# Loading the first constants ahead of the first q, with a new written-out order for ten steps

## The chip, the cores and the metric

The kernel runs on one core of a Trainium2 chip. The metric is the device time of one execution in microseconds. Times of the kernel before are the median of three runs; the profile and its trace come from one further execution of their own.

A core has five engines that the profile names PE (TensorE, matrix products), DVE (VectorE), ACT (ScalarE), POOL (GpSimd) and SP (SyncE, which here does nothing but issue transfers). PEld is the loading of a product's stationary operand. Each engine works through its own list of instructions in order; semaphores make one wait for another. A row "SPq" is the issue of a transfer, not the transfer.

## The reference

Two parts follow each other. The first is a gated linear recurrence, per batch and head, over 768 tokens with heads of 48 elements:

```python
batch, n_heads, seq, head_dim = (4, 8, 768, 48)
f = 1.0 / (1.0 + np.exp(-f_logit))
for t in range(S):
    state = f[:, :, t, :, None] * state + np.einsum('bhd,bhe->bhde', k[:, :, t], v[:, :, t])
    y[:, :, t] = np.einsum('bhd,bhde->bhe', q[:, :, t], state)
```

The second takes the 3072 tokens of 384 elements that come out, lets a gate choose one of eight experts for each, and runs that expert's two layers on it:

```python
logits = x @ w_gate
expert_idx = np.argmax(logits, axis=1)
...
    h = np.maximum(x_sorted[lo:hi] @ w1[e], 0.0)
    y_sorted[lo:hi] = h @ w2[e]
y = y_sorted[inv_perm]
return (gate_w[:, None] * y).astype(np.float32)
```

Everything is in 32-bit floats.

## The kernel before

**Units.** The recurrence is computed in chunks of 128 tokens. A unit is one chunk of two batches; there are twelve (NU = 12), and units alternate between two pairs of batches, so that unit u follows unit u - 2. A unit has 8 segments of 128 columns, in two halves a and b, one for each batch: four pairs of heads, with the two heads of a pair at partitions 0 and 64.

**Steps of a unit.** Each step has a short name, with the unit's number and, where it is done for half a unit, a or b behind it:

- lf, lk, lq, lv (SyncE): load f, k, q, v of the unit. f of units 0 and 1 is loaded in halves.
- exp, ln (ScalarE): the logarithms of the gates; sum (VectorE): their running sum (a scan); r and dec (ScalarE): the sum's exponential, and that of its negative.
- kr (POOL, L560): k times r. krv is the same product on VectorE. krx is kr with one dependency more: it also waits for the latest q, oh or place of VectorE that was written out ahead of it.
- q (VectorE, L583): q times dec.
- sc (TensorE, L594): scores k by q, 16 small products for a half, into two of four PSUM banks.
- mx, my (VectorE, L600): copy the scores under the causal mask, which frees the banks.
- kp (TensorE, L607): transposes of k against the identity; keep (ScalarE, L610) copies them out.
- wi (TensorE, L618): masked scores by v, into one of the two banks yt, one for each half. bef (L639): the old state's part, added into the same banks. set (ScalarE, L681) copies a bank out, after which the next unit's wi may begin in it.
- dp (TensorE, L655): what the unit adds to the state; upd (VectorE, L669 and L671) adds it, and updp (POOL, L673) scales it by the last decay, which last (POOL) has copied.
- xp (TensorE, L717): turns the output into rows and computes the gate's logits, against wx. lg (VectorE) sums the logits, lay (ScalarE) copies the rows.
- line (POOL), oh, place (VectorE), ex (ScalarE), send (POOL): choose the expert for a group of two units, count, find each row's place, and scatter the rows into the buffer xs with indirect transfers, two scatters for each send.

The results of kp, dp, xp and the counts take turns in two PSUM banks. Buffers for loads: four for q, three for k, two for f, three for v; three for the gates and decays.

**Constants.** `_consts()` packs all constants into one array fpack, of which the identity is the first 128 columns, and the mask into mpack. `load_first_consts()` (L164, step consts0) issues the transfers of the identity and the mask, 64 KB and 16 KB; `load_consts()` (L175, step consts1) those of the rest. The transposes kp need the identity as an operand; sel0 (L168, POOL) copies pieces of it into wx; the masks need mpack.

**Warm-up products.** `warm(count)` (L751, step fill) issues products of the cleared tile pad with itself into a bank that the first wi overwrites. Their result isn't used. Each is two records in the trace.

**The order.** Inside `tc.manual_schedule` each engine's instructions stand in the order in which they are written. For the first ten steps of the pipeline the order is written out by hand in the string FIRST_STEPS: a loop takes it word by word and calls what stands under that name in the table DO, with the unit and the half. A word sets its place only against the other words of its own engine. Units 10 and 11 and the end of the routing follow from the loop at L897, where ordered code takes the place of the words. Behind it stands the second part: the rows of each expert are read back from xs, turned, and multiplied by w1 and w2 (L337 and L353); the first two experts' first tiles are read back early, as soon as certain scatters have landed, and their products (PE s L337) begin inside the first part, near 117 us.

Of the kernel before, what the change touches and what calls it, by code (L numbers as in the profile page):

```python
# [121 lines left out]
def kernel(  # L122
# [305 lines left out]
    def load_pads(e):  # L428
# [12 lines left out]

    FIRST = 10
    FIRST_STEPS = """
        lf0a exp0a ln0a fill24 lf0b exp0b lk0 ln0b sum0a dec0a sum0b ends0 lf1a lq0 lf1b r0a
        r0b exp1a krv0a krv0b consts0 kp0a lk1 ln1a q0a sc0a lq1 exp1b ln1b dec0b keep0a
        sum1a sel0 fill8 dec1a r1a sum1b r1b kr1a q0b q1a kp0b kr1b keep0b lf2 lv0 lf3 lk2
        lv1 mx0a my0a lq2 sc0b mx0b my0b last0 dp0 upd0 sc1a exp2 ln2 wi0a gate0 lf4 kp1a
        dec1b lk3 lq3 lv2 kp1b ends1 sum2 ends2 q1b exp3 lf5 wi0b set0a keep1a last1 mx1a
        sc1b my1a mx1b r2 krx2 consts1 keep1b dp1 my1b wi1a set0b kp2a upd1 kp2b dec2 q2 ln3
        sum3 ends3 exp4 ln4 upd0p upd1p sc2a mx2a sc2b keep2a keep2b my2a last2 dec3 line0  # L450
        r3 xp0a xp0b set1a lq4 wi1b last3 lg0a lay0a mx2b my2b set1b wi2a wi2b dp2 lg0b krv3
        bef2 line1 line2 lk4 lv3 lf6 pads0 lk5 lv4 lay0b kp3a exp5 ln5 sum4 r4 q3 exp6 sc3a
        sc3b upd2 krx4 upd2p kp3b mx3a my3a keep3a xp1a dec4 mx3b my3b keep3b xp1b lg1a q4
        lg1b last4 lay1a dp3 sum5 lq5 lay1b sc4a sc4b ends4 ends5 oh1 kp4a upd3 lf7 set2a
        wi3a set2b wi3b mx4a my4a mx4b ln6 kp4b lk6 r5 kr5 dec5 q5 keep4a xp2a lv5 keep4b
        bef3 exp7 lg2a xp2b lay2a set3a set3b dp4 lq6 lf8 lk7 sum6 sc5a lg2b lay2b my4b
        ends6 dec6 upd4 ex1 place1 ln7 wi4a q6 sc5b lv6 r6 upd3p kp5a kp5b lq7 last5 last6
        mx5a kr6 lf9 wi4b lk8 lv7 keep5a line3 xp3a keep5b xp3b my5a sc6a mx5b upd4p my5b
        sc6b lg3a exp8 ln8 lay3a lg3b lay3b bef4 oh3 lq8 set4a lf10 set4b send5 sum7 r7 krx7
        dec7 last7 dp5 kp6a sum8 upd5 wi5a ends7 ends8 mx6a my6a mx6b wi5b bef5 kp6b line4  # L460
        lk9 keep6a xp4a keep6b q7 my6b set5a lv8 lq9 ex3 xp4b dec8 lg4a lg4b lay4a sc7a q8
        wi6a lay4b r8 place3 send6 dp6 upd6 kp7a sc7b mx7a my7a mx7b set5b line5 wi6b keep7a
        kp7b xp5a my7b krx8 sc8a exp9 ln9 keep7b xp5b exp10 ln10 lg5a sum9 lg5b oh5 lay5a
        lay5b lf11 bef6 upd5p last8 upd6p set6a set6b dp7 kp8a keep8a r9 wi7a upd7 kp8b
        keep8b lk10 sum10 kr9 mx8a my8a upd7p line6 xp6a lg6a ex5 sc8b ends9 exp11 mx8b dec9
        last9 q9 lay6a xp6b lg6b ends10 my8b lay6b place5 lv9 lq10 line7 dec10 q10 lk11
        last10 wi7b bef7 set7a set7b sc9a dp8 kp9a upd8 lv10 wi8a wi8b send7 r10 kr10 sc9b
        send8 lq11 lw0 lww0 lv11 lw1 ln11 mx9a lww1 kp9b keep9a keep9b upd8p xp7a xp7b send9
        bef8 my9a mx9b lg7a lay7a dp9 sum11 r11 lg7b lay7b my9b oh7 upd9
    """  # L470

    with ExitStack() as st:
# [891 lines left out]
```

## Time and profile before

| what | time |
|---|---|
| median of three runs | 391.99 us (391.94 to 394.16) |
| the profiled execution | 388.52 us |
| its span, first to last instruction | 386.5 us |
| first warm-up product starts | 1.57 us |
| first transpose kp0a starts | 11.03 us |
| last work of unit 9 (dp9) ends | 96.96 us |
| first expert product (PE s L337) starts | 117.50 us |

The page's rows of forty slices show how the engines share the span; a digit is the busy share of a slice in tenths, a slice is 9.66 us:

```profile
PE   8899999999999999999999999999999999999993
DVE  6899989897874632122121131116412113111360
ACT  6899885884532000010100110000010000001000
POOL 4444256658946310201002102100210210210112
```

The first part of the kernel takes the first twelve slices or so; there all four engines are used. From the thirteenth on TensorE works nearly alone, on the experts. Its granted clock has the digit 9 in all forty slices.

In the timeline rows below, the columns are the start in microseconds, the busy time, the engine with the line, operation and operands, the number of instructions merged into the row, and in brackets the idle time before it with what ended it. In rows of waits, the engine and line that waited stand left of the arrow, then what it waited for, with the total in microseconds, the number of waits and the longest.

### The profile page before, as it was taken

The page shows a single profiled execution, that of the slowest core. Times are in us where ns is not written, and L with a number is a line of the kernel's source. Part 1 is how long each engine was busy: PE and PEld are TensorE (multiplying, and loading weights), DVE is VectorE, ACT ScalarE, POOL GpSimd, SP SyncE. Part 2 cuts the span into 40 slices and gives each one's busy share as a digit, 9 for nine tenths or more (in the row PEclk, how much of TensorE's full clock was granted, in tenths as well). Part 3 has the DMA queues.
Part 4 walks back from the last instruction along what each step waited for, and adds up shares of the span by engine and source line. Part 5 has one row for each costly group of instructions (what it writes and reads, how often), then busy time and mean ns, then how long its engine had stood idle before and what let it go on. Part 6 is the DMA issues. An engine that isn't in the chain of part 4 may idle for free.

```text
span 386.5 us, 7693 instructions
## 1 busy us (share of the span) xinstructions
PE 377.2 (98%) x3054; PEld 264.6 (68%) x3054; DVE 170.2 (44%) x367; ACT 102.3 (26%) x190; POOL 98.9 (26%) x120
## 2 busy tenths in 40 slices
PE   8899999999999999999999999999999999999993
PEld 8789988889989777685555555654466466455452
DVE  6899989897874632122121131116412113111360
ACT  6899885884532000010100110000010000001000
POOL 4444256658946310201002102100210210210112
PEclk9999999999999999999999999999999999999999
DMA  7999765759993559594649999898163369993141
GB/s 260 388 360 372 261 230 199 249 181 303 412 354 123 174 162 333 118 344 77 197 130 396 264 392 395 221 398 220 41 247 113 102 211 385 397 415 138 21 175 54
DMA packets 51659, 94.81 MB, mean 245 GB/s; under 512 B 20840, under 2 KB 40875, under 8 KB 49568
## 3 DMA queue, kind: packets, MB, share of 16 engines
q1 hardware_dynamic: 48448, 84.62, 64.5%
q0 software_dynamic: 3168, 9.64, 6.6%
q8 instruction: 25, 0.41, 0.4%
q14 instruction: 18, 0.15, 0.1%
HBM read 79.23 MB, written 15.21 MB: 244 GB/s over the span
## 4 chain that ended last, share of the span: by engine, by line
PE 85%; DMA 6%; issue 2%; POOL 2%; DVE 1%; SPq 1%; ACT 1%; POOLq 0%; ACTq 0%; DVEq 0%
PE hps L337 28%; PE yps L353 24%; PE yps L1143 7%; PE s L594 5%; PE yt L618 4%; PE xp L717 3%; DMA xs<-xr,posi 3%; PE s L337 3%; PE hps L1117 3%; PE yp L353 3%; PE kp L607 2%; DMA fpack<-c_fpack 2%; PE dp L655 2%; PE yt L639 1%; DMA xrow<-xs 1%
## 5 line engine op out<-in xcount | busy, mean ns | idle before, releaser
L337 PE MATMUL hps<-xT,w1t 128*128 128x352 f32 (+2 forms) x384 | 110.1, 447 | 0.0
L337 PEld LDWEIGHTS hps<-xT,w1t 128*128 128x128 f32 x384 | 72.7, 190 | 37.2 <-issue 1.9
L353 PE MATMUL yps<-w2t,hT 128*128 128x384 f32 x288 | 94.4, 487 | 0.0
L353 PEld LDWEIGHTS yps<-w2t,hT 128*128 128x128 f32 x288 | 54.6, 190 | 38.6 <-issue 1.5
L196 POOL DMA_INDIRECT out_dram<-ysb,dst x24 | 23.4, 974 | 224.7 <-DVE ysb L364 215.6
L347 ACT ACTIVATE hT<-hps 128x352 f32<-128x352 f32 (+2 forms) x28 | 13.7, 491 | 200.7 <-PE hps L337 200.7
L349 DVE TENSOR_SCALAR hT<-hps 128x352 f32<-128x352 f32 (+2 forms) x28 | 15.6, 558 | 93.0 <-PE hps L337 93.0
L364 DVE TENSOR_SCALAR ysb<-yps,tg 128x384 f32<-128x384 f32 x22 | 13.6, 618 | 74.4 <-PE yps L353 55.7
L600 DVE COPY_PREDICATED at<-mpack,s 128x512 f32<-128x512 uint8 x48 | 32.1, 732 | 3.1 <-PE s L594 3.1
L560 POOL TENSOR_TENSOR k<-k,r 128x1024 f32<-128x1024 f32 (+1 forms) x11 | 25.2, 2296 | 20.5 <-ACT r L556 14.6
L542 DVE TENSOR_TENSOR_SCAN sum<-g,cap 128x1032 f32<-128x1032 f32 (+1 forms) x14 | 28.2, 2022 | 2.2 <-ACT g L535 2.2
L196 POOL DMA_INDIRECT xs<-xr,posi x24 | 25.5, 1063 | 13.7 <-issue 4.6
L1143 PE MATMUL yps<-qw,hqT 128*32 128x192 f32 (+1 forms) x192 | 26.8, 380 | 0.0
L594 PE MATMUL s<-q,k 64*128 64x128 f32 x384 | 26.3, 281 | 0.1
L717 PE MATMUL xp<-wx,ys 128*128 128x104 f32 x192 | 24.9, 279 | 0.2 <-ACT ys L681 0.2
L594 PEld LDWEIGHTS s<-q,k 64*128 64x128 f32 x384 | 22.8, 187 | 2.6 <-issue 1.2
L618 PE MATMUL yt<-at,v 128*48 128x128 f32 x384 | 24.3, 276 | 0.0
L717 PEld LDWEIGHTS xp<-wx,ys 128*128 128x128 f32 x192 | 22.9, 192 | 1.0 <-ACT ys L681 0.3
L618 PEld LDWEIGHTS yt<-at,v 128*48 128x48 f32 x384 | 20.2, 123 | 2.1 <-issue 1.0
L1143 PE MATMUL yps<-w2t,hT 128*32 128x384 f32 x192 | 21.4, 487 | 0.0
L583 DVE TENSOR_TENSOR q<-q,g 128x1024 f32<-128x1024 f32 (+1 forms) x14 | 16.7, 1196 | 1.1 <-DMA q<-in_qu_dram 0.9
L1143 PEld LDWEIGHTS yps<-w2t,hT 128*32 128x32 f32 x192 | 7.6, 110 | 13.0 <-issue 12.5
(116 smaller groups left out, 354.9 us busy)
## 6 DMA issues: line engine op xcount, KB each, us to landing
qw<-in_moe_w_dram SPq DMA_DIRECT2D x16, 1536.0 KB, 12.9
w1t<-in_moe_w_dram SPq DMA_DIRECT2D x8, 1536.0 KB, 7.3
w2t<-in_moe_w_dram SPq DMA_DIRECT2D x8, 1536.0 KB, 15.8
k<-in_ku_dram SPq DMA_DIRECT2D x12, 512.0 KB, 6.1
q<-in_qu_dram SPq DMA_DIRECT2D x12, 512.0 KB, 6.2
f<-in_fu_dram SPq DMA_DIRECT2D x10, 512.0 KB, 6.3
xs<-pad SPq DMA_DIRECT2D x8, 600.0 KB, 3.9
v<-in_vu_dram SPq DMA_DIRECT2D x12, 384.0 KB, 5.1
```

What stands on the lines that cost most here:

```text
L196: ins = nc.gpsimd.indirect_dma_start(out=dst, out_offset=bass.IndirectOffsetOnAxis(ap=idx, axis=0), in_=src, in_offset=None, bounds_check= ...
L337: nc.tensor.matmul(x["h"][:, f], lhsT=w[0][:, j, b * 128 : b * 128 + 128], rhs=x["xT"][:, j], start=j == 0, stop=j == KD - 1,)
L349: nc.vector.tensor_scalar(to, x["h"], 0.0, None, op0=OP.max)
L353: nc.tensor.matmul(yp, lhsT=x["hT"][:, f, t * C : t * C + C], rhs=w[1][:, f, :], start=f == 0, stop=f == NF - 1,)
L542: nc.vector.tensor_tensor_scan(x["sum"][:, part].rearrange("p s c -> p (s c)"), x["g"][:, part].rearrange("p s c -> p (s c)"), cap[:, part ...
L560: ins = on.tensor_tensor(k, k, units[u]["r"][:, part], op=OP.mult).ins
L583: return nc.vector.tensor_tensor(q, q, x["dec"][:, part], op=OP.mult).ins
L594: done["score"] = nc.tensor.matmul(ps[h][:, p], lhsT=x["k"][r, s], rhs=x["q"][r, s], start=True, stop=True).ins
L600: nc.vector.copy_predicated(x["at"][:, a, h], _bc(causal, 1, HP), x["ps", a][h])
L618: nc.tensor.matmul(x["yt"][a][DP * (h ^ a) : DP * (h ^ a) + D, p], lhsT=x["v"][:, a, 2 * p + h], rhs=x["at"][:, a, h, p], start=p == 0, st ...
L717: nc.tensor.matmul(x["xp", a][:, p], lhsT=x["ys", a][:, p], rhs=wx[:, p, 0:XW] if a else wx[:, p, E:WX], start=True, stop=True,)
L1143: nc.tensor.matmul(yp[r], lhsT=h[:, f, at : at + T], rhs=w[:, f, cols], start=f == 0, stop=f == NF - 1, skip_group_check=True,)
```

## The change

It replaces the string FIRST_STEPS and nothing else. The first lines of it:

```diff
-        lf0a exp0a ln0a fill24 lf0b exp0b lk0 ln0b sum0a dec0a sum0b ends0 lf1a lq0 lf1b r0a
-        r0b exp1a krv0a krv0b consts0 kp0a lk1 ln1a q0a sc0a lq1 exp1b ln1b dec0b keep0a
-        sum1a sel0 fill8 dec1a r1a sum1b r1b kr1a q0b q1a kp0b kr1b keep0b lf2 lv0 lf3 lk2
-        lv1 mx0a my0a lq2 sc0b mx0b my0b last0 dp0 upd0 sc1a exp2 ln2 wi0a gate0 lf4 kp1a
...
+        lf0a lf0b exp0a ln0a sum0a exp0b ln0b dec0a fill21 sum0b r0a lk0 krv0a r0b krv0b
+        lf1a consts0 lq0 lf1b kp0a dec0b q0a lk1 q0b sc0a exp1a ln1a sum1a exp1b ln1b sc0b
+        keep0a ends0 kp0b sum1b ends1 lq1 lf2 lv0 dec1a last0 r1a r1b lf3 lk2 lv1 lq2 fill8
+        q1a keep0b dp0 exp2 ln2 krx1a gate0 lf4 mx0a my0a mx0b my0b lk3 lq3 lv2 upd0 dec1b
...
```

Read by engine, this is what it does:

- SyncE: consts0 stands ahead of lq0 and lf1b instead of behind them. Its order is otherwise the same for all 58 steps.
- TensorE: 21 warm-up products at the start instead of 24. The eight others stand behind sc0b and kp0b instead of between sc0a and kp0b.
- The order on TensorE, VectorE, ScalarE and POOL is different in many places up to the last word. TensorE's for units 4 and 5, and ScalarE's around them:

```
before  PE   sc4a sc4b kp4a wi3a wi3b kp4b xp2a bef3 xp2b dp4 sc5a wi4a sc5b kp5a kp5b wi4b xp3a xp3b
after   PE   sc4a kp4a sc4b wi3a kp4b wi3b xp2a xp2b bef3 sc5a dp4 wi4a wi4b kp5a sc5b kp5b xp3a xp3b
before  ACT  exp5 ln5 r4 exp6 keep3a dec4 keep3b lay1a lay1b set2a set2b ln6 r5 dec5 keep4a keep4b exp7 lay2a set3a set3b lay2b
after   ACT  exp5 ln5 keep3a r4 keep3b dec4 lay1a set2a set2b lay1b exp6 dec5 keep4a r5 keep4b ln6 lay2a exp7 exp8 set3a set3b lay2b
```

- POOL: send7, the first send of the second group of units, stands ahead of kr9 instead of behind last9 and last10; send8 stands ahead of kr10 instead of behind it. Of the products k times r, those of unit 1 (both halves) and unit 6 wait in addition for VectorE's latest step (krx), those of units 2, 4 and 7 no longer do; unit 8's does in both.

No step is added or taken away apart from the three warm-up products.

More of the change, by code (lines that the diff above doesn't have):

```diff
@@ L443 @@
     FIRST_STEPS = """
-        lf0a exp0a ln0a fill24 lf0b exp0b lk0 ln0b sum0a dec0a sum0b ends0 lf1a lq0 lf1b r0a
-        r0b exp1a krv0a krv0b consts0 kp0a lk1 ln1a q0a sc0a lq1 exp1b ln1b dec0b keep0a
-        sum1a sel0 fill8 dec1a r1a sum1b r1b kr1a q0b q1a kp0b kr1b keep0b lf2 lv0 lf3 lk2
-        lv1 mx0a my0a lq2 sc0b mx0b my0b last0 dp0 upd0 sc1a exp2 ln2 wi0a gate0 lf4 kp1a
-        dec1b lk3 lq3 lv2 kp1b ends1 sum2 ends2 q1b exp3 lf5 wi0b set0a keep1a last1 mx1a
-        sc1b my1a mx1b r2 krx2 consts1 keep1b dp1 my1b wi1a set0b kp2a upd1 kp2b dec2 q2 ln3
@@ L450 @@
[L450 to L467, printed above, removed]
@@ L468 @@
-        send8 lq11 lw0 lww0 lv11 lw1 ln11 mx9a lww1 kp9b keep9a keep9b upd8p xp7a xp7b send9
-        bef8 my9a mx9b lg7a lay7a dp9 sum11 r11 lg7b lay7b my9b oh7 upd9
+        lf0a lf0b exp0a ln0a sum0a exp0b ln0b dec0a fill21 sum0b r0a lk0 krv0a r0b krv0b
+        lf1a consts0 lq0 lf1b kp0a dec0b q0a lk1 q0b sc0a exp1a ln1a sum1a exp1b ln1b sc0b
+        keep0a ends0 kp0b sum1b ends1 lq1 lf2 lv0 dec1a last0 r1a r1b lf3 lk2 lv1 lq2 fill8
+        q1a keep0b dp0 exp2 ln2 krx1a gate0 lf4 mx0a my0a mx0b my0b lk3 lq3 lv2 upd0 dec1b
@@ new lines @@
+        sc1a exp3 lf5 sum2 krx1b kp1a kp1b consts1 lq4 sel0 keep1a keep1b q1b ends2 wi0a
+        wi0b sc1b last1 r2 kr2 line0 mx1a my1a mx1b dp1 my1b line1 set0a set0b wi1a upd1
+        dec2 q2 ln3 exp4 wi1b sum3 kp2a sc2a mx2a kp2b sc2b my2a mx2b keep2a xp0a lg0a ln4
+        keep2b xp0b line2 dec3 lk4 lv3 set1a lay0a wi2a my2b r3 lg0b set1b dp2 lay0b last2
+        wi2b exp5 ln5 lf6 q3 pads0 krv3 kp3a sum4 keep3a sc3a sc3b upd0p r4 upd2 kp3b xp1a
+        keep3b ends3 mx3a my3a mx3b my3b lk5 dec4 lv4 lq5 ends4 lg1a xp1b lay1a bef2 set2a
@@ new lines @@
+        lg1b dp3 set2b upd1p lf7 q4 kr4 sc4a last3 lay1b kp4a upd2p sc4b lk6 lv5 exp6 sum5
+        lq6 wi3a upd3 kp4b wi3b oh1 dec5 q5 keep4a mx4a r5 xp2a lg2a lf8 last4 last5 ends5
+        my4a mx4b keep4b xp2b lg2b ln6 sum6 kr5 ends6 lk7 upd3p lay2a lv6 bef3 lq7 sc5a exp7
+        exp8 set3a set3b my4b dp4 lay2b dec6 ex1 wi4a wi4b upd4 place1 kp5a line3 last6 r6
+        krx6 q6 mx5a keep5a ln7 upd4p sc5b lf9 kp5b keep5b my5a send5 mx5b xp3a lg3a lay3a
+        xp3b bef4 set4a lg3b lay3b ln8 my5b oh3 sum7 sc6a set4b exp9 r7 dp5 upd5 line4 wi5a
@@ new lines @@
+        wi5b kp6a kp6b keep6a sc6b sum8 mx6a lk8 lv7 lq8 lf10 lk9 lv8 ex3 kr7 my6a keep6b
+        dec7 ln9 xp4a mx6b lg4a my6b xp4b lg4b lay4a lay4b send6 q7 bef5 dp6 dec8 lq9 place3
+        ends7 line5 line6 sc7a mx7a sc7b upd6 r8 kp7a my7a mx7b set5a krx8 wi6a last7 set5b
+        q8 keep7a kp7b upd5p xp5a my7b keep7b xp5b lg5a exp10 lg5b lay5a oh5 upd6p ends8
+        sum9 sc8a ln10 sum10 wi6b bef6 set6a lf11 set6b dp7 upd7 sc8b lay5b kp8a keep8a
+        last8 send7 mx8a wi7a lk10 lv9 wi7b bef7 r9 kr9 dec9 my8a mx8b kp8b dec10 upd7p lq10
@@ L470 @@
+        xp6a keep8b xp6b set7a wi8a r10 my8b lk11 lg6a lay6a ex5 q9 last9 lg6b lay6b ends9
+        ends10 lv10 lq11 q10 sc9a sc9b exp11 send8 place5 dp8 upd8 kp9a set7b ln11 kr10
+        last10 lw0 lww0 keep9a wi8b upd8p kp9b line7 xp7a lv11 lw1 mx9a my9a mx9b keep9b
+        lg7a lay7a bef8 sum11 xp7b r11 lg7b dp9 lay7b send9 my9b oh7 upd9 lww1
     """
```

## The prediction

> **What bounds the kernel now.** I read the page's busy rows first, then TensorE's own waits over the first 120 us, then the timeline of the first 16 us with the SyncE issues, and last the chain of waits near 117 us.
>
> ```profile
> PE 377.2 (98%) x3054; PEld 264.6 (68%) x3054; DVE 170.2 (44%) x367; ACT 102.3 (26%) x190; POOL 98.9 (26%) x120
> ```
> ```profile
> PE yt L754 <- DVE yt L482: 1.6, 1, 1.6
> PE kp L607 <- DMA fpack<-c_fpack: 1.4, 1, 1.4
> PE xp L717 <- ACT ys L681: 0.2, 1, 0.2
> PE s L337 <- DVE xT L320: 0.2, 1, 0.2
> ```
> TensorE is busy for 98% of the span, and these four rows are all its waits in the first 120 us: 1.6 us until a cleared bank is there, 1.4 us for the identity (fpack), and two of 0.2 us. From 11.03 us on it has no other gap. So this stage is worth what its first real product starts earlier, less any stall that the new order makes, and nothing else.
>
> ```profile
> 1.57 8.06 PE L754 MATMUL yt<-pad 128*128 128x128 f32 x48 [1.57 <-DVE yt L482]
> 2.14 0.43 SPq L517 DMA_DIRECT2D f<-in_fu_dram  x1
> 2.61 0.43 SPq L517 DMA_DIRECT2D q<-in_qu_dram  x1
> 3.09 0.43 SPq L517 DMA_DIRECT2D f<-in_fu_dram  x1
> 3.56 1.39 SPq L165 DMA_DIRECT2D fpack<-c_fpack  x1
> 4.99 0.65 SPq L166 DMA_DIRECT2D mpack<-c_mpack  x1
> 10.03 0.69 DVE L583 TENSOR_TENSOR q<-q,g 128x512 f32<-128x512 f32 x1 [0.87 <-DMA q<-in_qu_dram]
> 11.03 0.63 PE L607 MATMUL kp<-fpack,k 128*128 128x128 f32 x4 [1.40 <-DMA fpack<-c_fpack]
> 11.58 1.16 PE L594 MATMUL s<-q,k 64*128 64x128 f32 x16
> ```
> The transposes kp0a (L607) need the identity and start at 11.03; the first scores sc0a (L594) follow at 11.65 in the chain of waits. But sc0a's own operand, q0a, is ready at 10.72: VectorE took it up the moment q of unit 0 landed. Two transfers therefore end nearly together, and the change swaps them.
>
> **The change part by part.**
>
> *The swap.* Issue plus time to landing gives f1a at 8.75 (2.14 + 6.6), q0 at 10.0 (2.61 + 7.4), f1b at 10.7 (ScalarE's wait ends there), the identity at 10.89 (3.56 + 7.33), the mask at 11.1 (4.99 + 6.1). Landings follow the issues, with bytes moving at 350 to 400 GB/s. The identity came 0.17 us after f1b, the mask about 0.2 us later. In front of q0 they cost between 0.2 us (80 KB at 400 GB/s) and 0.37 us (those two steps). The other end: their issues take 1.39 + 0.65 = 2.04 us of SyncE, so q0 is issued near 4.7 instead of 2.61, and if the transfer engines ran dry it would land 2.04 us late. The stretches of 1 us show about 0.86 MB moved by 5.2 us, and 1.36 MB are issued ahead of q0 then, so they don't run dry. I take 0.32: q0 lands at 10.33, q0a is done at 10.33 + 0.69 = 11.02, sc0a starts at 11.06 (0.04 us for the hand-over, as at 25.56 in the chain), against 11.65: 0.59 us gained. Ends: 0.72 gained, 1.13 lost.
>
> *The identity and kp0a.* It lands at about 8.75 + 0.17 = 8.9. 21 products instead of 24 are six records fewer at the end of the warm-up, at 11 a microsecond: it ends near 9.63 - 0.55 = 9.1. kp0a then runs from 9.1 to 9.7, in the shadow of the wait for q0. Without that cover it costs its 0.63 us again. The three products are worth nothing themselves: they stood before a wait.
>
> *The clock.* The records of the warm-up go at 6 to 7 a microsecond until 6.5 us and at 10 to 12 from there; the row PEclk shows full clock throughout and doesn't tell this. [...] Here the release came 4.9 us after the first product, well before the 21st, and a gap of 1.40 us (9.63 to 11.03) was followed by transposes at 273 ns, which is full speed. The new gap, 9.7 to 11.06, is no longer. By the row: nothing. [...] I take the row.
>
> *Up to the second unit.* Old VectorE order q0a sum1a sum1b q0b q1a, new q0a q0b sum1a sum1b q1a: the same five pieces, 0.6 to 0.69 and 1.23 us each. They end at 10.33 + 4.35 = 14.7 (old 14.6), masks for unit 0 to 17.3 without the 0.35 us wait on sc0b that the timeline has at 16.29, sum2, q1b, masks of unit 1 and q2 to 25.1. TensorE from 11.06: sc0a, sc0b (q0b 11.6), kp0b, 8 warm-ups (1.97 us), dp0, sc1a at 16.9 (POOL's kr1a now waits for q1a, 14.7, and takes 1.4: 16.1), ..., sc2a at 25.9. Nothing is late, though VectorE is close. f1b lands 0.3 us later, and ln1b is done at 12.4, before sum1b at 12.8.
>
> *The rest of the ten steps.* Every step keeps its instructions; only orders differ. I laid TensorE's new list end to end with the times from start to start of the old timeline (scores 1.09, within 1.01, before 1.02, dp 1.07, transposes 0.57, rows 0.89 and 0.97), and VectorE's beside it. q is ready before its scores by 1.0 us for unit 4 (39.9 against 40.9), 4.7 for 5, 1.0 for 7, 1.6 for 8. Masks free banks 2 us or more ahead. SyncE's order differs in the constants alone, but a transfer still waits for its buffer: exp6 moves behind set2b and lay1b (about 41.4 instead of 34.96), so f of unit 8 is issued at 42.4 instead of 38.98, with k, v and q behind it in that queue. POOL: kr4, kr5, kr6, kr8, kr9 end 2 us or more ahead of their scores. The wait for VectorE's latest step (krx) goes from kr2, kr4 and kr7 and comes to kr1a, kr1b and kr6, where the identity copies (sel0, needed at 28.6, done near 19) and upd4p and send5 queue behind it; kr6 waits for place1 (53.8) and ends near 56.3, sc6a is at 58.8. I cost all this at 0; the cover is thin at the places named among the rivals.
>
> *The row chain near 117 us.* POOL is full from 81.30 to 106 us, after 5.95 us idle. Its scatters end in rows read back, whose transpose releases TensorE:
> ```profile
> 81.30 2.82 POOL L560 TENSOR_TENSOR k<-k,r 128x1024 f32<-128x1024 f32 x1 [5.95 <-ACT r L556]
> 102.94 1.84 POOL L196 DMA_INDIRECT xs<-xr,posi  x1 [0.17 <-issue]
> 117.50 2.27 PE L337 MATMUL s<-xT,w1t 128*128 128x128 f32 x18 [0.16 <-DVE xT L320]
> ```
> If this chain stayed, TensorE coming 0.59 us early would only wait longer. send7 (two scatters, 2.3 us) moves in front of kr9, into that idle time. kr11 then waits for r11 (about 98.2) instead of starting at 99.45: the chain comes 1.1 us early, more than TensorE's 0.59, and the 0.16 us goes too.
>
> Sum: 0.59 + 0.16 = 0.75, say 0.7 us. The profiled execution took 388.52 us with a span of 386.5; I expect a span of 385.8. The median of the three runs is 391.99, 3.5 above the profiled one, and the difference is put on that: 391.3.
>
> **The rivals.**
>
> *Small stalls give it back.* At kp3b, kp5b, kp7b and kp8b the new list has rows xp right behind. The second rows need ScalarE's copy of those transposes 0.89 us after they end, and the copy takes 0.55 to 0.59: 0.3 us to spare. The old list did this at kp9b (92.40) without a gap, for it; but ScalarE has r or dec in front of some of them, 0.95 us each, against it. Two places half a microsecond late: 391.99 - 0.7 + 1.0 = 392.3. Chance 0.2.
>
> *Slower: exp8 ahead of set3a.* The new ScalarE order is exp7 exp8 set3a. f of unit 8, issued at 42.4, must land by 49.9, that is within 7.5 us, or exp8 holds set3a, and wi4a on TensorE (51.7) waits. f took 5.7 to 7.2 us in this stage, for the change; q took 7.4 and up to 8.3 early on, against. Beyond 7.5 each microsecond is one lost; beyond 8.2 the kernel is slower than before. At 10 us: 391.3 + 2.5 = 393.8. Chance 0.12.
>
> *q0 lands 2 us late*, the other end of the swap: 391.99 + 1.13 - 0.16 = 393.0. The bytes still waiting at 5.2 us speak against it. Chance 0.08.
>
> *The change moves nothing*, since identity and q0 share the same engines and end together again: 391.99. Landings in order of issue speak against it. Chance 0.1.
>
> **How the numbers follow.** Forecast 0.45; the remaining 0.05 is for the clock and stalls I haven't seen. The forecast's own range is 391.0 to 391.9. I give 390.5 to 393.3: below, the most that all TensorE gaps can give (1.40 + 0.18 + 0.16 = 1.74, so 390.3) rounded in; above, the late q0 and a middling exp8 stall. About 1% (3.9 us) is what a measurement of this kernel can tell from no change. More than 1.74 us cannot come out of these gaps, so faster by 1% has 0.02, for the measurement alone; slower by 1% needs four microseconds of stalls, 0.06; within 0.92.
>
> **What would show it.** Right: the identity lands near 8.9, q0 near 10.3, kp0a about 9.1, sc0a about 11.1, no wait of TensorE until 117, where s L337 starts near 116.8 without waiting for xT. Wrong: sc0a after 11.65; a TensorE wait on ys (exp8) near 51.7 or on kn or lg behind a transpose; products at half speed after the gap; a wait on xT of over half a microsecond.

## The result, and the profile after

The change makes the kernel slower: 397.86 us (median of six runs, 396.81 to 398.52) against 391.97 us (six runs, 391.22 to 394.16), a ratio of 1.0139, interval 1.0113 to 1.0165. The profiled execution took 396.81 us with a span of 394.9, 8.4 us more than the one before. 391.3 us was forecast, with a range up to 393.3.

These are the page's rows of forty slices for the changed kernel, of 9.87 us each. TensorE has two dents that it hadn't, in the eighth slice (69.1 to 79.0 us) and the fourteenth (128 to 138), and the granted clock, full throughout before, falls in the ninth:

```profile
PE   8999999699999899999999999999999999999993
PEclk9999999989999999999999999999999999999999
```

TensorE's waits over the first 130 us of the changed kernel (who waited, for what, total in us, times, longest):

```profile
PE s L594 <- POOL k L560: 3.3, 1, 3.3
PE yt L754 <- DVE yt L482: 1.6, 1, 1.6
PE s L594 <- DVE q L583: 0.7, 1, 0.7
PE dp L655 <- issue: 0.6, 2, 0.4
PE dp L655 <- DMA v<-in_vu_dram: 0.4, 1, 0.4
```

The wait for the identity (1.4 us before) is gone; in its place stand 0.7 us for q0. So the front of the change works. But a wait of 3.3 us for k, which GpSimd multiplies, is new and larger than all that could be gained. The timeline of GpSimd in the changed kernel shows what held it:

```profile
65.88 1.04 POOL L196 DMA_INDIRECT xs<-xr,posi  x1 [0.16 <-issue]
67.22 1.81 POOL L196 DMA_INDIRECT xs<-xr,posi  x1 [0.30 <-issue]
69.02 0.21 POOL L566 COPY rend<-sum 128x8 f32<-128x8 f32 x1
75.59 0.19 POOL L702 COPY xr<-fpack 128x4 f32<-128x4 f32 x1 [6.35 <-DMA xs<-xr,posi]
75.71 0.15 POOL L703 MEMSET xr<- 128x56 f32 x1
75.82 2.33 POOL L560 TENSOR_TENSOR k<-k,r 128x1024 f32<-128x1024 f32 x1
78.11 0.19 POOL L578 COPY last<-g 128x8 f32<-128x8 f32 x1
```

L702 is step line6. It writes the token numbers into the row buffer xr of the fourth group of units. There are three such buffers (`bufs=3`), so the fourth group takes the first group's, and that is still the source of the scatters of send5 and send6. The last of these four scatters is issued at 67.22 and, by the chain of waits, lands 8.22 us later; until then line6 waits, 6.35 us. Behind it in GpSimd's queue stands krx8, and for that TensorE's scores sc8a wait, 3.27 us. Before the change line6 stood behind upd7p. The last scatter landed 5.7 us after its issue at 68.42 there, some 12 us before line6 began, and kr8 had run by then. From GpSimd's timeline of the kernel before:

```profile
71.14 2.37 POOL L560 TENSOR_TENSOR k<-k,r 128x1024 f32<-128x1024 f32 x1 [1.03 <-DVE xr L275]
85.87 0.22 POOL L702 COPY xr<-fpack 128x4 f32<-128x4 f32 x1
```

TensorE's timeline of the changed kernel, before and behind that wait:

```profile
72.91 2.03 PE L717 MATMUL xp<-wx,ys 128*128 128x104 f32 x16
78.21 1.42 PE L594 MATMUL s<-q,k 64*128 64x128 f32 x16 [3.27 <-POOL k L560]
79.57 1.95 PE L618 MATMUL yt<-at,v 128*48 128x128 f32 x16
81.44 1.52 PE L639 MATMUL yt<-q,state 48*48 48x128 f32 x32
82.90 1.14 PE L655 MATMUL dp<-v,kn 128*64 128x48 f32 x32
```

The three groups behind the wait take 1.42, 1.95 and 1.52 us where the same groups take 1.16, 1.08 and 1.09 elsewhere: 1.56 us more. The view of stretches, with TensorE's busy time (and instructions), the granted clock, the transfer engines' share and GB/s, tells why; the changed kernel:

```profile
74.00:78.00 4.00, 0.94 (x8) 1.00 0.41 136
78.00:80.00 2.00, 1.79 (x20) 0.74 0.00 0
80.00:82.00 2.00, 2.00 (x28) 0.50 0.00 0
82.00:84.00 2.00, 2.00 (x62) 0.90 0.65 183
```

In steps of half a microsecond the mean clock is 0.97 in the step from 78.5, 0.50 in the six that follow and 0.62 in the step from 82.0. So TensorE had half its clock from 78.97 to 82.38 us, 3.41 us. The wait is paid for twice: while it lasts, and in the slow work behind it.

In the two profiled executions the last work of unit 9 ends at 102.67 instead of 96.96 us, 5.7 later; the wait and the slow work behind it make 4.8 of that. The other 2.7 us of the span come later: 1.5 in the fourteenth slice, where TensorE waits for ScalarE's hT (the experts' first-layer output), the rest in small gaps. The experiments tell whether those belong to the change.

### The profile page after: what moved, and what is told of

Same layout as the page of the kernel before. It is cut to its first block, busy times and chain, and to the rows that moved or that the text cites. A ratio compares the mean times of both kernels' runs of the same rounds, so it can differ in the third digit from the quotient of the medians.

```text
span 394.9 us, 7686 instructions
## 1 busy us (share of the span) xinstructions
PE 379.7 (96%) x3048; PEld 266.2 (67%) x3048; DVE 172.6 (44%) x367; ACT 102.3 (26%) x190; POOL 112.1 (28%) x120
## 4 chain that ended last, share of the span: by engine, by line
PE 87%; DMA 5%; POOL 3%; issue 2%; DVE 0%; ACT 0%; SPq 0%; POOLq 0%
PE hps L337 28%; PE yps L353 24%; PE yps L1143 7%; PE s L594 5%; PE yt L618 5%; PE xp L717 4%; PE s L337 3%; PE yp L353 3%; PE hps L1117 3%; PE yt L639 2%; DMA xs<-xr,posi 2%; PE kp L607 2%; PE dp L655 2%; DMA v<-in_vu_dram 2%; DMA f<-in_fu_dram 1%
## 5 line engine op out<-in xcount | busy, mean ns | idle before, releaser
L196 POOL DMA_INDIRECT xs<-xr,posi x24 | 30.7, 1279 | 16.5 <-issue 4.6
L618 PE MATMUL yt<-at,v 128*48 128x128 f32 x384 | 25.3, 281 | 0.2 <-ACT ys L681 0.2
L618 PEld LDWEIGHTS yt<-at,v 128*48 128x48 f32 x384 | 20.9, 126 | 2.2 <-issue 1.1
```

The costliest lines, as they stand in the source:

```text
L196: ins = nc.gpsimd.indirect_dma_start(out=dst, out_offset=bass.IndirectOffsetOnAxis(ap=idx, axis=0), in_=src, in_offset=None, bounds_check= ...
L618: nc.tensor.matmul(x["yt"][a][DP * (h ^ a) : DP * (h ^ a) + D, p], lhsT=x["v"][:, a, 2 * p + h], rhs=x["at"][:, a, h, p], start=p == 0, st ...
```

## The experiments

Theory A: line6's wait for its buffer, with kr8 queued behind it, is the loss. Rival B: the many other moves of the order lose the time. The ratios are to the kernel before, run on the same chip beside each group of runs; its median was 387.6 to 388.2 us there. Where an expectation gives a time, it was reckoned from the 391.97 and 397.86 above, so it is the ratio or the difference that can be compared.

**line6 moved back.** The changed kernel with one word in its old place.

```diff
-        ends7 line5 line6 sc7a mx7a ...
+        ends7 line5 sc7a mx7a ...
-        ... kp8b dec10 upd7p lq10
+        ... kp8b dec10 upd7p line6 lq10
```

> The changed kernel with one word moved: line6 stands behind upd7p again, as before the change, no longer in front of krx8. Theory A (the buffer wait: line6 takes the third and last buffer of the rows, so GpSimd waits in it until the scatters of the first group have landed, with kr8 queued behind): the 6.3 us wait of GpSimd on its scatter and TensorE's 3.3 us wait on kr8 go, the granted clock stays at full speed near 80 us, and the time falls by 5 us or more from the 397.9 of the changed kernel, to 391 to 392.5. Rival B (the many other moves of the order lose the time, and kr8 would be late anyway): TensorE still waits for k or q near 75 us, and the time stays above 395.

Measured: 386.93 us, ratio 0.998 (0.9955 to 1.0005). Its waits of TensorE over the whole execution:

```profile
PE yt L754 <- DVE yt L482: 1.6, 1, 1.6
PE s L594 <- DVE q L583: 1.0, 1, 1.0
PE dp L655 <- DMA v<-in_vu_dram: 0.4, 1, 0.4
PE xp L717 <- ACT ys L681: 0.2, 1, 0.2
```

The wait on GpSimd's k is gone, and so are the hT wait of the fourteenth slice and the small gaps. One word out of some 420 makes the whole loss; B falls. Nor do the other moves gain anything that shows.

**The wait taken away by a buffer.** The order untouched, a fourth buffer for the rows. That alone doesn't fit: the kernel's pool then takes 74.28 KB of each partition, and 69.41 are left. To make room, one buffer for the experts' turned rows and rows of 392 elements.

```diff
-group["xr"] = wk.tile([128, n, ROW], F32, tag="xr", name="xr", bufs=3)
+group["xr"] = wk.tile([128, n, ROW], F32, tag="xr", name="xr", bufs=4)
...
-x["xT"] = ep.tile([128, KD, TILES * C], F32, name="xT")[:, :, 0 : x["rows"]]
+x["xT"] = ep.tile([128, KD, TILES * C], F32, name="xT", bufs=1)[:, :, 0 : x["rows"]]
...
-TOK, GATE, USED, ROW = DM, DM + 1, DM + 2, DM + 16
+TOK, GATE, USED, ROW = DM, DM + 1, DM + 2, DM + 8
```

> The changed kernel, order untouched, with four buffers for the rows instead of three; to make room the turned rows of the experts (xT) have one buffer instead of two and a row is 392 elements instead of 400. Theory A: line6 finds a free buffer, GpSimd doesn't wait on its scatter, TensorE not at sc8a, and the trace up to 100 us looks like that with line6 moved back: unit 9's dp ends near 96. The ratio to before is 0.995 to 1.003 unless the single xT costs something in the second part. Rival B: TensorE waits 2 us or more near 75 us all the same.

Measured: 386.84 us, ratio 0.997 (0.9952 to 0.9989). GpSimd's timeline in this run, for the same steps as above:

```profile
66.50 0.98 POOL L196 DMA_INDIRECT xs<-xr,posi  x1 [0.30 <-issue]
67.48 0.21 POOL L566 COPY rend<-sum 128x8 f32<-128x8 f32 x1
67.61 0.19 POOL L702 COPY xr<-fpack 128x4 f32<-128x4 f32 x1
67.74 0.12 POOL L703 MEMSET xr<- 128x24 f32 x1
68.56 2.36 POOL L560 TENSOR_TENSOR k<-k,r 128x1024 f32<-128x1024 f32 x1 [0.70 <-PE s L594]
```

line6 in the very same place costs 0.19 us when its buffer is free, and TensorE has no wait for kr8. It is the buffer, not the place.

**line6 alone moved in the kernel before.**

```diff
-        kp7b mx7a my7a mx7b set5b line5 wi6b ...
+        kp7b mx7a my7a mx7b set5b line5 line6 wi6b ...
-        ... upd7p line6 xp6a ...
+        ... upd7p xp6a ...
```

> The kernel before with line6 alone moved, to the place in front of krx8 that the change gives it. Theory A: GpSimd waits there for the landing of the scatters near 68 us, until about 76, kr8 ends near 79 instead of 73.5, the scores of unit 8 (74.7 in the old trace) wait about 4 us, the clock falls for a while, and the time rises by 4 to 7 us, to 396 to 399. Rival B: within 1.5 us of before.

Measured: 392.69 us, ratio 1.0138 (1.0104 to 1.0172): the loss of the whole change, from one word. In its profile the wait of TensorE is only 2.5 us, smaller than expected, but the clock stays down for longer. The view of stretches for this run:

```profile
74.00:76.00 2.00, 0.14 (x2) 1.00 0.87 291
76.00:78.00 2.00, 2.00 (x22) 0.82 0.56 222
78.00:80.00 2.00, 2.00 (x32) 0.50 0.03 11
80.00:82.00 2.00, 2.00 (x40) 0.50 0.26 55
82.00:84.00 2.00, 2.00 (x20) 0.50 0.54 215
84.00:86.00 2.00, 2.00 (x25) 0.97 0.00 0
```

Half a clock from 77.3 to 84.12 us, 6.8 us and so twice as long as in the changed kernel's profile. Half of that, 3.4 us, is an estimate of what the clock took, more than the wait did.

**line6 one place later, behind krx8.**

```diff
-        ends7 line5 line6 sc7a ... set5a krx8 wi6a
+        ends7 line5 sc7a ... set5a krx8 line6 wi6a
```

> The changed kernel with line6 moved by one place, behind krx8 instead of in front of it. Theory A (what counts is what queues behind the waiting instruction): GpSimd still waits on its scatter until about 76, for 3 us or so, but kr8 has gone ahead and ends near 73, TensorE doesn't wait at sc8a, the clock stays up, and the ratio to before is 0.996 to 1.003. Rival (the wait itself costs, since last7, upd5p and the sends behind it are late as well): exp10 on ScalarE waits for last7, the scores or rows near 85 to 100 are late, and the ratio is over 1.006.

Measured: 388.07 us, ratio 0.9978 (0.9959 to 0.9996), as A expects. But the ratio leaves out the three longest of its 22 runs, and the other 19 spread from 386.7 to 391.06 us; the longest of these is the profiled one. There the rival shows. ScalarE's exp10 waits for last7, which stands behind line6 on GpSimd and ends at 77.79, and lay5a waits behind exp10. (The row names VectorE's sum, the later of two events by this profile; in the changed kernel's profile the same wait, 4.58 us, is put to last7.) The timeline of ScalarE in this run, then one row of TensorE's waits:

```profile
77.83 1.06 ACT L527 ACTIVATE g<-f 128x1024 f32<-128x1024 f32 x1 [4.88 <-DVE sum L542]
78.79 0.19 ACT L527 ACTIVATION_READ_ACCUMULATOR g<-f 128x1 f32 x1
78.88 0.46 ACT L743 COPY xr<-xp 128x384 f32<-128x384 f32 x1
```
```profile
PE dp L655 <- ACT xr L743: 2.1, 1, 2.1
```

Behind these 2.1 us the granted clock falls here too, to 0.99 from 78 to 80 us, 0.50 from 80 to 82 and 0.66 from 82 to 84, which makes 3.4 us at half; A had not expected that. So kr8 is the first step hurt by the wait and not the only one. In the kernel before, line6 doesn't wait for these scatters, and its 58 runs beside these spread from 386.9 to 392.4 us, so the spread alone doesn't tell how often the stall occurs.

**The clock by itself.** 16, and in another run 26, products of the cleared tile in front of sc8a, into the bank that sc8a overwrites. line6's wait stays.

```diff
+    HOT = 16
...
+            for _ in range(HOT if (u, a) == (8, 0) else 0):
+                nc.tensor.matmul(
+                    ps[0][:, 0], lhsT=pad[:, 0:C], rhs=pad[:, 0:C], start=True, stop=True
+                )
             for p, h, r in heads():
```

> The changed kernel with 16 products of the cleared tile added in front of the scores sc8a, into the bank that these overwrite; TensorE runs them while it waits for kr8, whose wait behind line6 stays. Theory A with the clock as second part: TensorE's wait of 3.3 us is filled by 16 products at 0.19 us, the granted clock stays at full speed from 78 to 83 us where it fell to a half, and the time falls by about 1.7 us against the changed kernel, a ratio to before near 1.009 to 1.010 instead of 1.014. If the fall of the clock is no part of the loss, the ratio stays at 1.014.

> As the run with 16 products in front of sc8a, but with 26, about 4.9 us of work: in its profile kr8 came so late that TensorE still stood for 2.3 us after the 16 and the clock fell all the same. Theory A with the clock as second part: with 26 TensorE has no gap of 1 us or more before sc8a, the granted clock stays at full speed to 86 us, and the ratio to before is at or under that with 16 (1.005), although 10 products more are run. If the clock is no part of it, each product over the wait costs 0.19 us: 1.008 or more.

> The changed kernel, unchanged, on the chip of the runs that follow and with more executions. Theory A: a ratio to before of 1.012 to 1.016 again; the profile shows the wait on the scatter in front of line6, the wait at sc8a and the fall of the clock behind it. The wait of 1.5 us near 131 us on ScalarE's hT and the gaps of 0.4 us in dp5 and dp8, which the first profile has and the kernel with line6 moved back has not, are chance if they are missing here, and belong to the change if they come again.

Measured: the changed kernel again, on the chip of these runs, 391.64 us, ratio 1.0092 (1.0062 to 1.0123); with 16 products 390.29, 1.005 (1.0031 to 1.0069); with 26 products 392.44, 1.0104 (1.0072 to 1.0136). With 26 TensorE doesn't wait at all there and the clock stays at 1.00 from 70 to 90 us. The timeline of TensorE in that run, then in the changed kernel run again:

```profile
73.61 5.99 PE L594 MATMUL s<-pad 128*128 128x128 f32 x52
79.53 1.16 PE L599 MATMUL s<-q,k 64*128 64x128 f32 x16
80.62 1.08 PE L623 MATMUL yt<-at,v 128*48 128x128 f32 x16
```
```profile
76.90 2.08 PE L594 MATMUL s<-q,k 64*128 64x128 f32 x16 [3.25 <-POOL k L560]
78.91 1.64 PE L618 MATMUL yt<-at,v 128*48 128x128 f32 x16
80.47 1.09 PE L639 MATMUL yt<-q,state 48*48 48x128 f32 x32
```

Behind 5.9 us of filler the scores take 1.16 us at a clock of 1.00; behind a wait of 3.25 us they take 2.08, and the next group 0.56 more, at 0.50 from 77 to 80 us. 26 were too many: each took 0.23 us, not 0.19, and their 5.9 us cost more than the 3.25 waited and the 1.5 lost to the clock. That run misses its expectation, and by its own words it would speak for the rival; the two timelines show that it doesn't, since the filler took 1.2 us more than the wait and the slow work together, and unit 9 ends 1.2 us later than in the changed kernel (101.50 against 100.34 us). With 16 the ratio is lower than expected, 1.005 instead of 1.009 to 1.010, but the changed kernel run beside it is lower too. Between these two it falls by 0.0042, 1.6 us. 16 products at 0.23 us instead of 4.7 us of waiting and slow work would give 1.0, and the two intervals overlap. (The profiled execution with 16 was the second longest of its 22, 394.28 us, with kr8 stretched to 4.35 us, a gap of 2.3 us left and the clock at 0.59 and 0.56 in the two stretches from 80 to 84 us, so it doesn't show the case that was meant.) The dropping of the clock is shown by the views; its price in the whole time is supported, not settled.

The changed kernel's second profile has the wait on the scatter (6.3 us), the wait at sc8a and the half clock, and neither the hT wait nor the gaps in dp. Those were chance in the first: from the first expert product to the last product of TensorE it takes 265.8 us there, and 263.1 in this profile and in that of every other version.

Why the ratio was 1.0139 in the first runs and 1.0092 here stays open; the intervals overlap. How long the clock stays down is one candidate: half speed for one stretch of 3.41 us lowers the mean of 395 us by 0.0043, two by 0.0086, and one or two are what the profiles show. But the mean clocks of the six first runs of the changed kernel (0.987 to 0.993) and of the eight here (0.988 to 0.997) overlap.

**The front alone.** The kernel before with the constants in front of q0 and 21 products, all else in the old order.

```diff
-        lf0a exp0a ln0a fill24 ... lf1a lq0 lf1b r0a
-        r0b exp1a krv0a krv0b consts0 kp0a ...
+        lf0a exp0a ln0a fill21 ... lf1a consts0 lq0 lf1b r0a
+        r0b exp1a krv0a krv0b kp0a ...
```

> The kernel before with the first part of the change alone: the identity and mask in front of q0 and f1b, 21 warm-up products; all other words in their old order. By the prediction's sum: q0 lands within 0.4 us of the old 10.0, the first scores start at 11.1 or earlier instead of 11.65, TensorE has no new wait, and the time is 0.4 to 1.3 us under that of before. Rival: VectorE, busy all through 10 to 25 us, holds TensorE's gain back within the first two units, and the time is that of before within 0.3 us.

> The kernel before, unchanged, for a second profile: does the landing of q0, the identity and f1b in its order of loads repeat (10.0, 10.9 and 10.7 us in the first profile), or does it vary by a microsecond, as one profile with the same loads suggests (q taken up at 8.83)? If it repeats, the swap gains what the first profile shows, 1.3 us at the first scores; if it varies, the first profile was a late one and the gain of the swap is smaller on most runs.

Measured: 387.21 us, ratio 0.9972 (0.9956 to 0.9988), 1.1 us gained, which beats both kernels. q0 is taken up at 9.76 and the first scores start at 10.51. Unit 9 ends at 96.11 us, against 96.96 and 96.27 in the two profiles of the kernel before. The first expert product, which waits for xT in both of those and not here, starts at 116.33, against 117.50 and 117.14. Beside it the second profile of the kernel before, both as timelines:

```profile
9.76 0.69 DVE L583 TENSOR_TENSOR q<-q,g 128x512 f32<-128x512 f32 x1 [0.87 <-DMA q<-in_qu_dram]
10.51 1.16 PE L594 MATMUL s<-q,k 64*128 64x128 f32 x16 [1.11 <-DVE q L583]
```
```profile
9.37 0.69 DVE L583 TENSOR_TENSOR q<-q,g 128x512 f32<-128x512 f32 x1 [0.59 <-DMA q<-in_qu_dram]
10.37 0.63 PE L607 MATMUL kp<-fpack,k 128*128 128x128 f32 x4 [1.48 <-DMA fpack<-c_fpack]
10.93 1.16 PE L594 MATMUL s<-q,k 64*128 64x128 f32 x16
```

The landings vary. With q0 in front it is taken up at 10.03, 9.37 and, in the run with line6 alone moved, 8.83, and the first scores start at 11.58, 10.93 and 10.19. With the constants in front they start between 9.80 and 10.51 in nine profiles. The means, 10.90 and 10.20, are 0.7 us apart, near the 0.59 of the sum. With three profiles that differ by 1.4 us among themselves this is an indication, and it shrinks: at the start of sc2a, the first scores of unit 2, the means are 24.90 and 24.61.

**v of unit 0 earlier,** in the version with line6 moved back:

```diff
-        ... kp0b sum1b ends1 lq1 lf2 lv0 dec1a
+        ... kp0b sum1b ends1 lq1 lv0 lf2 dec1a
```

> The version with line6 moved back, and v of unit 0 loaded in front of f of unit 2 instead of behind it: TensorE's wait of 0.4 us for v0 at dp0 goes. If TensorE's lead is kept, the ratio to before falls by 0.001 to 0.996 or 0.997; if VectorE, which is busy all through 10 to 25 us, is what holds it there, nothing moves: 0.997 to 0.998.

Measured: 386.97 us, ratio 0.9978 (0.9964 to 0.9991); nothing moves. dp0 starts without a wait, but f of unit 2 is later, sum2 with it, and TensorE waits 0.5 us for q at sc1b instead; sc2a starts at 24.88 us, against 24.78 without the step.

## Why the prediction was wrong

**The step that failed** is "The rest of the ten steps": "I cost all this at 0", and in it "POOL: kr4, kr5, kr6, kr8, kr9 end 2 us or more ahead of their scores". kr8 ended at 78.17, and its scores stood 3.3 us. I had checked what each product waits for, and which semaphore waits the krx steps add. For line6, a copy of 0.2 us that moves past krx8, I checked neither its buffer nor what stands behind it. The copy's cost was therefore put at nothing without a reason. The change adds a wait there of 6.3 us, with kr8, last7, the updates and a send queued behind it, and the old trace shows no such wait, since line6 came 12 us after the landing then. But it has the time from issue to landing, 5.7 us, from which the wait could have been foreseen.

**The clock.** The sum took the row PEclk, full throughout, and at the place in question, the gap before the first scores, that was right: in the profile before, transposes behind a gap of 1.40 us go at 273 ns, the median of all 80 in that trace, and in all twelve profiles the first scores take 1.16 us for a half or 2.06 for both. But the price of a stall left the clock out. In five profiles it was at half for 3.4 us (after waits of 2.1, 2.3, 3.25 and 3.3 us) or 6.8 us (after one of 2.5). Half of 3.4 us, 1.7, is an estimate of what one such stretch takes; behind the waits of 3.25 and 3.3 us the work took 1.5 and 1.56 us more.

**The swap** was right in mechanism, and its size came near partly by luck: 0.59 forecast; 0.7 between the means of the first scores, 1.1 (0.5 to 1.7) in the whole time, of which a part comes only at the wait on xT. The 0.32 us by which q0 was to land later don't show: on the mean it is taken up at 9.41 us with q0 in front and at 9.46 behind the constants. The sum set 11.06 against 11.65 from the chain; the first scores start at 11.58 in the timeline, so it should have given 0.52. It also took the late warm-up records at 11 a microsecond, where a record that crosses the edge of a stretch is counted twice; they go at about 9 (the 52 of the run with 26 products took 5.99 us). The first profile, on which the sum stood, was a late one of its kind: the first scores vary by 1.4 us with q0 in front and by 0.7 with the constants in front. I hadn't seen that dp0 would then wait 0.4 us for v0, nor, as the last experiment shows, that taking this wait away would win nothing, as VectorE's next steps then come later.

**The row chain near 117 us.** TensorE waits for xT in the two profiles of the kernel before, 0.2 and 0.5 us, and in no other. That goes for the front alone too, which keeps send7 in its old place. So the chain was not as stiff as I took it for, and what I gave as the cause of its coming earlier isn't shown. It was also worth more than 0.16 us: from the end of unit 9 to the first expert product it takes 20.5 and 20.9 us in the two profiles of the kernel before, and 20.2 to 20.3 in all the others.

**The rivals.** exp8 in front of set3a cost nothing: exp8 started at 47.83 and wi4a followed without a wait. Nor did the transposes with rows close behind. The bound on gains, 1.74 us, held. The range failed because every slow case in it was a stall of one to 2.5 us, with no clock behind it.

## What to carry to other kernels

When an instruction is moved earlier, ask when the buffer that it writes comes free, even if the instruction itself takes 0.2 us: a buffer that a scatter reads from came free here at the landing, 8.2 us after the issue. Then look at what stands behind it in its queue. And price a TensorE stall like those here, of 2.1 to 3.3 us, at more than its length: the work behind them ran at half clock for 3.4 or 6.8 us, so that 3.3 us of waiting cost 4.8, and 2.5 an estimated 5.9.

## What the runs showed of the hardware

- After TensorE waits of 2.1 to 3.3 us, in five profiles, the granted clock fell to 0.50, in four for 3.4 us and in one for 6.8. The fall began 0.2 us before to 1.4 us after work was taken up again. It didn't come after gaps of 1.0 to 1.5 us: behind the longest of them, 1.51 us for hT in the changed kernel, the clock was 1.00 from 128 to 140 us. Why it stayed down for 6.8 us in one profile, in which TensorE was busy throughout that stretch, is open.
- The last of the scatters that line6 waits for took 8.22 us from issue to landing in the changed kernel's profile and 6.11 with line6 alone moved (both by the chain of waits). In the four other profiles in which line6 waits, its start came 7.1 to 8.1 us after the issue. In the kernel before it took 5.7 us.
- The same loads in the same order, from the same first issue at 0.75 us, brought q0 to its use at 8.83, 9.37 or 10.03 us in three profiles.
